# Eight-batch pooled attention and channel mix: longer weight slots, a planner with other rules, and a new order of the first hundred microseconds

## The chip, the cores and the metric

The kernel runs on one core of one Trainium2 chip. The core has a matrix engine (PE, with its weight loads shown as PEld), three engines for elementwise work (DVE, ACT, POOL) and a queue engine (SP) that issues nearly all transfers. The metric is the device time of one execution in microseconds (us); lower is better. The kernel before took 605.85 us, the median of three runs (605.77 to 607.02).

## The reference

```python
# attention, for 8 batches x 8 heads, q/k/v of 576 x 64
k_p = k.reshape(B, H, Sp, pool, D).mean(axis=3)      # 576 keys pooled to 72
v_p = v.reshape(B, H, Sp, pool, D).mean(axis=3)
scores = scale * np.matmul(q, k_p.transpose(0, 1, 3, 2))
attn = softmax(scores)                               # over the 72 pooled keys
x = heads_to_columns(np.matmul(attn, v_p))           # (8, 576, 512)
# channel mix
x_prev = x shifted down by one token, zero at each batch's start
xk = mu_k * x + (1.0 - mu_k) * x_prev
xr = mu_r * x + (1.0 - mu_r) * x_prev
k = np.maximum(xk @ w_k, 0.0)                        # 512 -> 1024
v = k * k @ w_v                                      # 1024 -> 512
r = 1.0 / (1.0 + np.exp(-(xr @ w_r)))                # 512 -> 512
return r * v
```

The three weights arrive as 64-bit floats.

## The kernel before

The 4608 tokens are cut into 12 chunks of 384, and each chunk into 3 tiles of 128 tokens. A tile goes through `softmax` (scores by `products`, maximum, exponential, sum, normalization) and is transposed on PE (`transposed`, `transposed_rest`) for chunks 0 and 1, or through a transfer to DRAM and back for later chunks. A chunk then goes through `attended` (the product with the pooled values), `shifted` (the two mixes, xk and xr), `hidden` (8 column blocks of w_k, relu, square), `gate` (w_r, sigmoid) and `mixed` (w_v, times the gate).

Chunk 0 multiplies with 32-bit weights in PE's plain fp32 form (the tile names begin with got_). Chunks 1 to 11 split weights and operands into a high and a low part and do three faster products in their place (names w_k, w_r, w_v; xkh and xkl). So each of the 20 weight pieces (wk0 to wk7, wr0 to wr3, wv0 to wv7) is first loaded as 64-bit words, then made a 32-bit one by `convert` (a cast on the engine that TOP_BY names, then a DVE operation, line 631), and later split by `split` (HIGH_BY and LOW_BY name the engines).

Keys and values are summed over groups of 8 by `sums`, on PE with the identity (line 672), on DVE or on POOL (SUM_BY). `warm` and `fill` run matmuls whose results nobody reads. BY_HEAD names the tiles whose exponentials are 8 instructions on ACT, each with its own sum (line 817); the others take one DVE subtraction (825), one ACT exponential (830) and one DVE sum (832).

The order of all instructions is made when the kernel is built, by the class `Order`. Every piece of work is a thread with a due time (DUE, by name); a cost model keeps a clock for each engine, estimates when loads land (`fetched`) and how fast PE's clock runs (`stretch`), and always issues, among those that could start about first, the thread that is due first. Nothing of the model is left at run time: each engine executes its list in order and waits on semaphores. Loads leave on SP in the order of LOADS, with eight in flight. A weight piece lies in one of 21 slots: `sb.tile([P, 2 * WP + 1], I32)`, 4100 bytes a partition.

Of the kernel before, what the change touches and what calls it, by code (L numbers as in the profile page):

```python
# [10 lines left out]
I32 = mybir.dt.int32  # L11
# [8 lines left out]
P = 128  # L20
# [11 lines left out]
WP = 512  # L32
# [9 lines left out]
    "k0 k1 q0 q1 wk0 wk1 q2 r0 v0 q4 wr2 v1 v2 q5 wr3 c0 wk7 k2 wk3 wv4 wv6 q3 k3 wk5 wv2 wk2 "  # L42
    "wv7 wv1 v3 wr1 wr0 r1 wv5 wv0 wk4 wv3 wk6 "
)

SUM_BY = {"k0": "t", "k1": "v", "v0": "t", "v1": "t", "r0": "v", "k2": "t", "k3": "t", "v2": "t", "v3": "g", "r1": "g", "k5": "v", "k4": "v", "v5": "v", "r2": "v", "v4": "g"}

NORM_BY = {0: "g", 1: "g", 2: "g", 3: "v", 7: "v", 5: "v", 4: "g", 8: "g", 6: "v"}
# [3 lines left out]
TOP_BY = {"k": "aaaaaaaa", "r": "vvvv", "v": "aaagaaga"}  # L52
HIGH_BY = {"k": "aaaaaagg", "r": "aaga", "v": "gaaaaaga"}
LOW_BY = {"k": "vvgvgggv", "r": "vgvg", "v": "gvvgvvvv"}
BY_HEAD = (0, 1, 5, 7, 8)

SQUARED_ON_ACT = 4
# [27 lines left out]
    "warm": 490.04, "constants": 16.13, "complements": 481.25, "values 2 1": 205.94, "values 2 0": 224.51,  # L85
# [123 lines left out]
class Order:  # L209
# [75 lines left out]
    def stretch(self, at, length):  # L285
# [7 lines left out]
        elif busy > 0.93:  # L293
            self.slow = False
# [1052 lines left out]
```

## Time and profile before

| | |
|---|---|
| median of three runs | 605.85 us |
| the profiled execution | 607.92 us, of which 606.1 us is the span from the first to the last instruction |
| PE busy | 594.3 us, 98% of the span |
| DVE, ACT, POOL busy | 60%, 53%, 34% |
| granted PE clock, mean | 0.994 |
| chain of waits that ended last | PE 86%, DVE 3%, ACT 3%, POOL 2% |

The busy digits of the page stand for 40 equal slices of about 15 us. The granted clock is a share of 2.4 GHz: 1.00 is that level and 0.50 is 1.2 GHz. An idle engine matters only where somebody waits for it. In the first 10 us the clock row prints 0.9 and more whatever PE does; how fast it runs there has to be read from the durations.

### The profile page before, as it was taken

The numbers are of one execution on the slowest core, as the hardware profiler recorded it, in microseconds if no ns is written. First come the engines' busy times: TensorE is split into PE (matmuls) and PEld (weight loads), VectorE is DVE, ScalarE is ACT, GpSimd is POOL, SyncE is SP. The second block draws the span as 40 slices with busy tenths as digits, with TensorE's granted clock in tenths as the row PEclk, the third lists the DMA queues.
The fourth block names the chain that finished last, engine by engine and source line by source line (L and its number), as shares of the span: only waits on it lengthen the run. The fifth ranks groups of instructions, "written<-read, shape, count | busy, mean of one in ns | idle before, by whom it ended". The sixth has DMA issues, their size and how long they took to land.

```text
span 606.1 us, 10539 instructions
## 1 busy us (share of the span) xinstructions
PE 594.3 (98%) x4026; PEld 494.1 (82%) x4026; DVE 362.1 (60%) x738; ACT 318.7 (53%) x670; POOL 207.7 (34%) x295
## 2 busy tenths in 40 slices
PE   7799999999999999999999999999999999999997
PEld 7655545978987988978988988987987988978985
DVE  4688877986985836667936736664864324423411
ACT  4668775575457455565556446365566336344420
POOL 0234338347036228147206208217425006005000
PEclk9979999999999999999999999999999999999999
DMA  9995044358464206416324106424014000000001
GB/s 304 382 379 182 31 158 111 115 151 238 131 160 115 75 32 167 165 72 171 129 79 111 58 21 147 155 92 114 19 41 113 18 1 35 18 0 37 18 1 52
DMA packets 43011, 66.62 MB, mean 110 GB/s; under 512 B 7504, under 2 KB 23120, under 8 KB 42960
## 3 DMA queue, kind: packets, MB, share of 16 engines
q1 hardware_dynamic: 42816, 65.82, 34.6%
q8 instruction: 31, 0.51, 0.4%
q14 instruction: 20, 0.16, 0.1%
q10 hardware_dynamic: 144, 0.13, 0.1%
HBM read 47.65 MB, written 18.28 MB: 109 GB/s over the span
## 4 chain that ended last, share of the span: by engine, by line
PE 86%; DVE 3%; ACT 3%; POOL 2%; issue 1%; DVEq 0%; POOLq 0%; ACTq 0%
PE mm L1126 32%; PE mm L1212 31%; PE mm L1179 15%; PE pair L1038 3%; PE pair L739 2%; PE pair L1019 2%; ACT e L817 1%; POOL xkl L1098 1%; POOL xrl L1098 1%; PE mm L672 1%; ACT turned L622 1%; DVE ptr L974 0%; POOL w_r L657 0%; DVE w_k L657 0%; ACT sh L1139 0%
## 5 line engine op out<-in xcount | busy, mean ns | idle before, releaser
L1126 PE MATMUL mm<-xkh,w_k 128*128 128x384 f32 x704 | 181.7, 339 | 0.0
L1212 PE MATMUL mm<-w_v,sh 128*128 128x512 f32 x528 | 170.5, 397 | 0.0
L1126 PEld LDWEIGHTS mm<-xkh,w_k 128*128 128x128 f32 x704 | 127.5, 188 | 2.3 <-issue 1.0
L1212 PEld LDWEIGHTS mm<-w_v,sh 128*128 128x128 f32 x528 | 99.1, 188 | 27.8 <-issue 5.0
L1126 PE MATMUL mm<-xkl,w_k 128*128 128x384 f32 x352 | 118.7, 337 | 0.3 <-POOL xkl L1098 0.3
L1212 PE MATMUL mm<-w_v,sl 128*128 128x512 f32 x264 | 104.1, 394 | 0.0
L1080 DVE SCALAR_TENSOR_TENSOR xm<-pair,mu_sb,t 128x384 f32<-128x384 f32 x88 | 51.8, 613 | 83.7 <-POOL t L1071 47.3
L1179 PE MATMUL mm<-w_r,xrh 128*128 128x512 f32 x264 | 84.3, 394 | 0.0
L844 POOL TENSOR_TENSOR e<-e,sm 128x576 f32<-128x576 f32 x28 | 33.5, 1206 | 143.9 <-DVE sm L839 99.3
L1139 ACT ACTIVATE rk<-mm 128x384 f32<-128x384 f32 x88 | 43.1, 491 | 70.4 <-PE mm L1126 65.3
L1147 DVE SCALAR_TENSOR_TENSOR rk<-mm,rk 128x384 f32<-128x384 f32 x88 | 48.1, 553 | 35.3 <-ACT rk L1139 35.1
L1126 PEld LDWEIGHTS mm<-xkl,w_k 128*128 128x128 f32 x352 | 66.1, 188 | 0.6 <-POOL xkl L1098 0.6
L1154 ACT CAST sh<-rk 128x384 fp32r<-128x384 f32 x88 | 44.7, 512 | 36.5 <-DVE rk L1147 36.2
L1098 POOL TENSOR_TENSOR xkl<-xm,xkh 128x384 fp32r<-128x384 f32 x44 | 47.7, 1086 | 46.7 <-ACT xkh L1096 46.6
L1060 ACT ACTIVATE t<-pair,om_sb 128x384 f32<-128x384 f32 x96 | 49.3, 580 | 27.4 <-PE pair L1038 26.6
L657 DVE TENSOR_TENSOR sl<-rk,sh 128x384 fp32r<-128x384 f32 x88 | 50.0, 573 | 16.6 <-ACT sh L1154 15.7
L1212 PEld LDWEIGHTS mm<-w_v,sl 128*128 128x128 f32 x264 | 49.5, 188 | 11.3
L1179 PEld LDWEIGHTS mm<-w_r,xrh 128*128 128x128 f32 x264 | 49.6, 188 | 11.1
L1225 DVE TENSOR_TENSOR rs<-mm,rs 128x512 f32<-128x512 f32 (+1 forms) x37 | 24.8, 673 | 56.1 <-PE mm L1212 55.7
L1179 PE MATMUL mm<-w_r,xrl 128*128 128x512 f32 x132 | 52.1, 395 | 0.0
L1098 POOL TENSOR_TENSOR xrl<-xm,xrh 128x384 fp32r<-128x384 f32 x44 | 47.7, 1089 | 5.1 <-ACT xrh L1096 4.8
L657 POOL TENSOR_TENSOR stage<-stage 128x512 f32<-128x512 f32 (+5 forms) x54 | 47.0, 873 | 3.8 <-ACT rs L1185 1.9
(106 smaller groups left out, 710.2 us busy)
## 6 DMA issues: line engine op xcount, KB each, us to landing
qs<-in_qT SPq DMA_DIRECT2D x36, 256.0 KB, 4.5
out<-rs SPq DMA_DIRECT2D x35, 256.0 KB, 2.0
passing<-pm SPq DMA_DIRECT2D x30, 288.0 KB, 2.1
stage<-in_kT SPq DMA_DIRECT2D x14, 576.0 KB, 4.0
turned<-passing SPq DMA_DIRECT2D x40, 192.0 KB, 3.8
stage<-in_vm SPq DMA_DIRECT2D x13, 512.0 KB, 4.1
got_wk<-in_w_k SPq DMA_DIRECT2D x8, 512.0 KB, 8.7
got_wv<-in_w_v SPq DMA_DIRECT2D x8, 512.0 KB, 10.5
```

The source lines that it names most:

```text
L657: (nc.vector if on_vector else nc.gpsimd).tensor_tensor(out=out, in0=a, in1=b, op=op)
L844: eng.tensor_tensor(out=e, in0=e, in1=sm.broadcast_to([P, 2, 4, KEYS]), op=ALU.mult)
L1060: nc.scalar.activation(out=t[:, m, 1:n + 1], in_=xp, func=AF.Copy, scale=om_sb[:, m, g:g + 1])
L1080: nc.vector.scalar_tensor_tensor(out=xm[:, :n], in0=xp, scalar=mu_sb[:, m, g:g + 1], in1=t[:, m, :n], op0=ALU.mult, op1=ALU.add,)
L1098: nc.gpsimd.tensor_tensor(out=lo, in0=xm[:, :n], in1=hi, op=ALU.subtract)
L1126: nc.tensor.matmul(out=hp, lhsT=w[:, o], rhs=x[:, ct, o_t], start=(ct == 0 and k == 0), stop=(ct == NCT - 1 and k == len(terms) - 1),)
L1139: nc.scalar.activation(out=rk[:, :n], in_=hp, func=AF.Relu)
L1147: nc.vector.scalar_tensor_tensor(out=rk[:, :n], in0=hp, scalar=0.0, in1=rk[:, :n], op0=ALU.max, op1=ALU.mult)
L1154: nc.scalar.copy(out=sh, in_=rk[:, :n])
L1179: nc.tensor.matmul(out=bank, lhsT=x[:, ct, o], rhs=w, start=(ct == 0 and k == 0), stop=(ct == NCT - 1 and k == len(terms) - 1),)
L1212: nc.tensor.matmul(out=bank, lhsT=s[:, o], rhs=w, start=(jt == 0 and k == 0), stop=(jt == NJT - 1 and k == len(terms) - 1),)
L1225: nc.vector.tensor_tensor(out=rs[:, o], in0=bank[:, o], in1=rs[:, o], op=ALU.mult)
```

## The change

The slot of a weight piece becomes 2 * WP + 32 words, 4224 bytes. The model in `Order` is changed: loads are limited to eight in flight with another latency, rate and a lag; PE's clock is judged by fixed slices of time, with 64-row matmuls counted as a quarter; clears and the casts of `convert` have other prices. LOADS, the tables that give work to engines, and 171 of 481 due times (those of the first three or four chunks) are replaced, and four due times are new. The other 310 are the same numbers.

```diff
 LOADS = (
-    "k0 k1 q0 q1 wk0 wk1 q2 r0 v0 q4 wr2 v1 v2 q5 wr3 c0 wk7 k2 wk3 wv4 wv6 q3 k3 wk5 wv2 wk2 "
-    "wv7 wv1 v3 wr1 wr0 r1 wv5 wv0 wk4 wv3 wk6 "
+    "k0 k1 q1 wk1 q0 wk0 r0 q5 v0 q2 v1 wr2 v2 wr3 wk7 k2 q4 wv4 c0 wv6 q3 k3 wk3 wv1 wv2 wk5 wk2 wv7 wv3 "
+    "v3 wr1 wr0 wk4 wv5 r1 wv0 wk6 "
 )
-NORM_BY = {0: "g", 1: "g", 2: "g", 3: "v", 7: "v", 5: "v", 4: "g", 8: "g", 6: "v"}
+NORM_BY = {0: "v", 1: "v", 2: "g", 3: "g", 7: "v", 5: "v", 4: "v", 8: "v", 6: "v", 10: "g", 11: "g", 9: "g"}
-TOP_BY = {"k": "aaaaaaaa", "r": "vvvv", "v": "aaagaaga"}
-HIGH_BY = {"k": "aaaaaagg", "r": "aaga", "v": "gaaaaaga"}
-LOW_BY = {"k": "vvgvgggv", "r": "vgvg", "v": "gvvgvvvv"}
-BY_HEAD = (0, 1, 5, 7, 8)
-SQUARED_ON_ACT = 4
+TOP_BY = {"k": "ggagaaaa", "r": "avvv", "v": "vaagaagv"}
+HIGH_BY = {"k": "gaaaaaga", "r": "agaa", "v": "gaaaagaa"}
+LOW_BY = {"k": "vvggvgvg", "r": "vggg", "v": "vvvggvvv"}
+BY_HEAD = (0, 7, 12, 14)
+SQUARED_ON_ACT = 8
 DUE = {
-    "keys 0 0": 144.96, "values 0 0": 154.97, "keys 0 1": 673.65, "values 0 1": 197.76,
+    "keys 0 0": -36.14, "values 0 0": 113.89, "keys 0 1": 721.88, "values 0 1": 519.26, "last_values 0": 287.88,
...
-    WINDOW = 3.4
+    WINDOW = 3.413
+    PHASE = 1.0
+    LAG = 1.7
...
-        self.landed = max(self.now - 0.6 + 2.5, self.landed) + kb / 380.0
-        self.make(what, self.landed)
+        at = self.now
+        if len(self.landings) >= 8:
+            at = max(at, self.landings[-8])
+        self.landed = max(at - 0.6 + 2.25, self.landed) + kb / 400.0
+        self.landings.append(self.landed + (self.LAG if 13 < self.landed < 50 else 0.0))
+        self.make(what, self.landings[-1])
...
-            got = sb.tile([P, 2 * WP + 1], I32, name=f"got_{kind}{i}", tag=f"w{slot}")
+            got = sb.tile([P, 2 * WP + 32], I32, name=f"got_{kind}{i}", tag=f"w{slot}")
```

The first place is PE between the sums of batch 0's values and the first `attended` (L1019 before, L1018 now; every line of the changed file from there on stands one lower). `early_sl`, `early_xrl` and `turned_99` hold raw values and keys, `pm` and `px` are normalized tiles, `pair` holds scores or the attended product. Before:

```order
L672 MATMUL mm_116<-early_sl,ident 128x128 x8
L672 MATMUL mm_114<-early_sl,ident 128x128 x8
L963 MATMUL mm_116<-ident,px_90 64x128
L672 MATMUL mm_115<-early_xrl,ident 128x128 x4
L963 MATMUL mm_114<-ident,px_90 64x128
L672 MATMUL mm_115<-early_xrl,ident 128x128 x4
L926 MATMUL mm_115<-ident,pm_88 128x128 x4
L672 MATMUL mm_117<-turned_99,ident 128x144 x4
L926 MATMUL mm_115<-ident,pm_87 128x128 x4
L672 MATMUL mm_117<-turned_99,ident 128x144 x4
L963 MATMUL mm_115<-ident,px_91 64x128
L926 MATMUL mm_117<-ident,pm_88 128x128 x4
```

and now, the same stretch with the row of scores and the first row of the attended product behind it:

```order
L671 MATMUL mm_116<-early_sl,ident 128x128 x8
L671 MATMUL mm_114<-early_sl,ident 128x128 x8
L671 MATMUL mm_115<-early_xrl,ident 128x128 x8
L962 MATMUL mm_114<-ident,px_90 64x128
L962 MATMUL mm_117<-ident,px_89 64x128
L925 MATMUL mm_115<-ident,pm_88 128x128 x4
L962 MATMUL mm_115<-ident,px_91 64x128
L925 MATMUL mm_114<-ident,pm_88 128x128 x4
L925 MATMUL mm_117<-ident,pm_87 128x128 x4
L671 MATMUL mm_114<-turned_99,ident 128x144 x4
L738 MATMUL pair_113<-ks_69,qs_105 64x72 x16
L1018 MATMUL pair_112<-ptr_316,vbd_r_73 128x384 x2
```

Four of the eight key sums that stood between the transposes have moved behind the first attended product, and the transposes of all three tiles stand together after the value sums.

The second place is ACT from its first weight cast to the copies of the same transposes (L622 and L621 are the cast of `convert`, L817 and L816 the exponentials by head, L971 and L970 copies of the transposed rest, L933 and L932 of the transposed tile). Before:

```order
L622 CAST turned_98<-got_wk_132 128x512
L622 CAST turned_98<-got_wk_135 128x512
L817 ACTIVATE e_85,sm_95<-pair_112,mx_93 128x72 x8
L817 ACTIVATE e_86,sm_96<-pair_113,mx_94 128x72 x8
L703 COPY vs_71<-mm_116 128x128
L830 ACTIVATE e_85<-e_85 128x576
L703 COPY vs_71<-mm_114 128x128
L971 CAST ptr_302<-mm_116 32x128 x2
L971 CAST ptr_302<-mm_114 32x128 x2
L703 COPY vs_72<-mm_115 128x128
L622 CAST turned_98<-got_wk_240 128x512
L980 CAST ptr_302<-mm_114 32x128
```

and now:

```order
L816 ACTIVATE e_85,sm_95<-pair_112,mx_93 128x72 x8
L829 ACTIVATE e_86<-e_86 128x576
L702 COPY vs_71<-mm_116 128x128
L829 ACTIVATE e_85<-e_85 128x576
L702 COPY vs_71<-mm_114 128x128
L621 CAST turned_98<-got_wk_222 128x512
L702 COPY vs_72<-mm_115 128x128
L970 CAST ptr_316<-mm_114 32x128
L970 CAST ptr_316<-mm_117 32x128
L970 CAST ptr_316<-mm_114 32x128
L970 CAST ptr_316<-mm_117 32x128
L932 COPY pt_338<-mm_115 128x4x128
```

The casts of wk0 and wk1 and eight of the sixteen exponentials have left ACT, and the cast of wk7 (got_wk_222, a load) now stands ahead of the last value copy and of all the transposes' copies.

## Rows read from the trace of the kernel before

**Rows 1.** The page: busy time of each engine, and PE's granted clock.
```profile
PE 594.3 (98%) x4026; PEld 494.1 (82%) x4026; DVE 362.1 (60%) x738; ACT 318.7 (53%) x670; POOL 207.7 (34%) x295
...
PEclk9979999999999999999999999999999999999999
```
**Rows 2.** Busy time by stretch: stretch, its length, engines, granted clock, DMA share, GB/s.
```profile
22.50:26.20 3.70, 2.28 (x17) 1.74 (x15) 3.59 (x11) 2.11 (x7) 0.00 (x0) 1.00 1.02 408
26.20:29.60 3.40, 2.30 (x18) 1.92 (x17) 3.32 (x8) 2.91 (x7) 1.79 (x2) 1.00 1.03 400
29.60:33.05 3.45, 1.96 (x44) 1.11 (x42) 2.70 (x6) 2.03 (x8) 0.00 (x0) 1.00 1.04 413
33.05:39.87 6.82, 6.82 (x29) 3.91 (x22) 5.72 (x13) 5.83 (x10) 0.71 (x7) 0.50 1.03 383
39.87:60.00 20.13, 19.88 (x128) 11.97 (x127) 16.75 (x29) 14.33 (x43) 11.01 (x14) 1.00 0.65 232
60.00:150.00 90.00, 89.55 (x651) 62.01 (x650) 72.63 (x145) 58.62 (x141) 46.45 (x59) 1.00 0.45 133
150.00:600.00 450.00, 450.00 (x2939) 392.09 (x2938) 246.86 (x509) 222.63 (x415) 144.43 (x204) 1.00 0.27 79
```
**Rows 3.** PE in order of time to 62 us: start, length, instruction, idle before.
```profile
3.08 2.08 PE L524 MATMUL mm<-turned 128*128 128x256 f32 x4 [3.08 <-DVE turned L520]
4.94 4.05 PE L672 MATMUL mm<-stage,ident 128*128 128x144 f32 x16
...
9.93 1.23 PE L739 MATMUL pair<-ks,qs 64*64 64x72 f32 x64
11.09 4.73 PE L540 MATMUL mm<-ident 128*128 128x128 f32 x40
15.75 0.73 PE L739 MATMUL pair<-ks,qs 64*64 64x72 f32 x32
...
18.93 2.05 PE L672 MATMUL mm<-early_sl,ident 128*128 128x128 f32 x16 [0.47 <-DMA early_sl<-in_vm]
...
27.53 1.15 PE L672 MATMUL mm<-turned,ident 128*128 128x144 f32 x8
...
31.98 0.62 PE L1019 MATMUL pair<-ptr,vbd_r 96*128 96x384 f32 x2 [0.86 <-ACT ptr L980]
...
38.08 2.42 PE L1126 MATMUL mm<-xkh,got_wk 128*128 128x384 f32 x4
...
56.78 5.43 PE L1126 MATMUL mm<-xkh,got_wk 128*128 128x384 f32 x16 [0.25 <-DVE sh L1147]
```
**Rows 4.** ACT in order of time to 64 us, same columns.
```profile
12.32 0.32 ACT L817 ACTIVATE e<-pair,mx 128x72 f32<-128x72 f32 x1 [0.70 <-DVE mx L813]
...
16.78 0.41 ACT L817 ACTIVATE e<-pair,mx 128x72 f32<-128x72 f32 x1
...
23.59 0.77 ACT L622 CAST turned<-got_wk 128x512 f16<-128x512 bf16 x1 [0.30 <-DMA got_wk<-in_w_k]
...
25.81 0.26 ACT L980 CAST ptr<-mm 32x128 fp32r<-32x128 f32 x1
...
26.40 0.59 ACT L933 COPY pt<-mm 128x512 f32<-128x512 f32 x1
```
**Rows 5.** DVE in order of time to 64 us, same columns.
```profile
2.54 0.48 DVE L520 MEMSET turned<- 128x512 f32 x1
...
27.20 1.60 DVE L722 TENSOR_TENSOR vbd_r<-vq,mask_sb 96x256 fp32r<-96x256 f32 x2
```
**Rows 6.** PE in order of time from 60 to 160 us, same columns.
```profile
84.02 0.69 PE L1019 MATMUL pair<-ptr,vbd_r 96*128 96x192 f32 x4 [0.19 <-ACT e L817]
...
104.92 0.44 PE L1126 MATMUL mm<-xkl,w_k 128*128 128x384 f32 x1 [0.26 <-POOL xkl L1098]
```
**Rows 7.** ACT in order of time from 64 to 92 us, same columns.
```profile
71.26 1.28 ACT L1185 ACT_TABLE_LOAD   x1
72.55 0.60 ACT L1185 ACTIVATE rs<-mm 128x512 f32<-128x512 f32 x1
```

More of the change, by code (lines that the diff above doesn't have):

```diff
@@ L41 @@
 LOADS = (
-    "k0 k1 q0 q1 wk0 wk1 q2 r0 v0 q4 wr2 v1 v2 q5 wr3 c0 wk7 k2 wk3 wv4 wv6 q3 k3 wk5 wv2 wk2 "
-    "wv7 wv1 v3 wr1 wr0 r1 wv5 wv0 wk4 wv3 wk6 "
-)
-SUM_BY = {"k0": "t", "k1": "v", "v0": "t", "v1": "t", "r0": "v", "k2": "t", "k3": "t", "v2": "t", "v3": "g", "r1": "g", "k5": "v", "k4": "v", "v5": "v", "r2": "v", "v4": "g"}
-NORM_BY = {0: "g", 1: "g", 2: "g", 3: "v", 7: "v", 5: "v", 4: "g", 8: "g", 6: "v"}
+    "k0 k1 q1 wk1 q0 wk0 r0 q5 v0 q2 v1 wr2 v2 wr3 wk7 k2 q4 wv4 c0 wv6 q3 k3 wk3 wv1 wv2 wk5 wk2 wv7 wv3 "
+    "v3 wr1 wr0 wk4 wv5 r1 wv0 wk6 "
+)
+SUM_BY = {"k0": "t", "k1": "v", "v0": "t", "v1": "t", "r0": "v", "k2": "t", "k3": "t", "v2": "t", "v3": "v", "r1": "g", "k5": "v", "k4": "v", "v5": "v", "r2": "v", "v4": "g"}
+NORM_BY = {0: "v", 1: "v", 2: "g", 3: "g", 7: "v", 5: "v", 4: "v", 8: "v", 6: "v", 10: "g", 11: "g", 9: "g"}
 WARMING = 4
 FILLS = ((("scored", 1), 20),)
-TOP_BY = {"k": "aaaaaaaa", "r": "vvvv", "v": "aaagaaga"}
-HIGH_BY = {"k": "aaaaaagg", "r": "aaga", "v": "gaaaaaga"}
-LOW_BY = {"k": "vvgvgggv", "r": "vgvg", "v": "gvvgvvvv"}
-BY_HEAD = (0, 1, 5, 7, 8)
-SQUARED_ON_ACT = 4
+TOP_BY = {"k": "ggagaaaa", "r": "avvv", "v": "vaagaagv"}
[3 more added lines that the diff above has]
+SQUARED_ON_ACT = 8
 REST_BY = (1, 1, 3)
@@ L62 @@
 DUE = {
[22 rows of a table removed]
-    "warm": 490.04, "constants": 16.13, "complements": 481.25, "values 2 1": 205.94, "values 2 0": 224.51,
[17 rows of a table removed]
[22 rows of a table added]
+    "warm": 525.34, "constants": -181.8, "complements": 1678.53, "values 2 1": -741.97, "values 2 0": 598.55,
[15 rows of a table added]
     "x_parts 3 2 1 0": 735.71, "x_parts 3 3 0 0": -119.85, "x_parts 3 3 1 0": -10.57, "hidden 3 0 0": 6.06,
@@ L105 @@
     "split_turned 6": 410.72, "split_turned 7": 501.45, "split_turned 8": 495.95, "split_turned 9": 313.38,
-    "free_turned": 478.83, "fetch_turned 2": 92.93, "split_turned 10": 300.71, "split_turned 11": 198.56,
[14 rows of a table removed]
+    "free_turned": 478.83, "fetch_turned 2": -381.2, "split_turned 10": 300.71, "split_turned 11": 198.56,
[12 rows of a table added]
     "softmax 27": -756.46, "scores 9": 168.64, "softmax 28": 531.98, "softmax 29": 732.89,
@@ L218, in __init__ @@
         self.landed = 0.0
+        self.landings = []
         self.now = 0.0
@@ L224, in __init__ @@
         self.mode = "whole"
-        self.slow, self.bursts = True, []
+        self.busy = {}
         self.counts = {}
@@ L283, in advance, with stretch @@
                 return
-    def stretch(self, at, length):
+    def stretch(self, at, length, mode):
         if at > 60:
             return length
-        self.bursts = [b for b in self.bursts if b[1] > at - self.WINDOW]
-        busy = sum(b[1] - max(b[0], at - self.WINDOW) for b in self.bursts) / self.WINDOW
-        if busy < 0.39:
-            self.slow = True
-        elif busy > 0.93:
-            self.slow = False
-        length *= 1 + self.slow
-        self.bursts.append((at, at + length))
+        k = int((at + self.PHASE) / self.WINDOW)
+        if self.busy.get(k - 1, 0.0) < 0.6:
+            length *= 2
+        weight = 0.25 if mode == "quarters" else 1.0
+        end = at + length
+        while at < end:
+            until = min(end, (k + 1) * self.WINDOW - self.PHASE)
+            self.busy[k] = self.busy.get(k, 0.0) + weight * (until - at) / self.WINDOW
+            at, k = until, k + 1
         return length
@@ L332, in run @@
                     length, self.mode = length + self.CHANGE[mode], mode
-                length = self.stretch(at, length)
+                length = self.stretch(at, length, mode)
             elif func and func[0] and func[0] != self.table:
@@ L518, in warm @@
         zeros = yield take("tmp")
-        yield "dve", 0.6, False
+        yield "dve", 0.5, False
         nc.vector.memset(zeros, 0.0)
@@ L528, in cleared @@
     def cleared(i):
-        yield "dve", 0.6, False
+        yield "dve", 0.5, False
         nc.vector.memset(tops[i], 0.0)
@@ L614, in convert @@
         got = held.pop(("got", kind, i))
-        words = got[:, 1:].rearrange("p (n two) -> p n two", two=2)[:, :, 0]
-        first = got.bitcast(BF16)[:, 2:].rearrange("p (n four) -> p n four", four=4)[:, :, 2]
+        words = got[:, 1:2 * WP + 1].rearrange("p (n two) -> p n two", two=2)[:, :, 0]
+        first = got.bitcast(BF16)[:, 2:4 * WP + 2].rearrange("p (n four) -> p n four", four=4)[:, :, 2]
         top = yield take("tmp")
@@ L620, in convert @@
         if by == "a":
-            yield act(WP)
+            yield "act", 0.62, False
             nc.scalar.copy(out=upper, in_=first)
         elif by == "g":
-            yield pool(WP)
+            yield "pool", 0.91, True
             nc.gpsimd.tensor_copy(out=upper, in_=first)
         else:
-            yield dve(WP)
+            yield "dve", 0.42, True
             nc.vector.tensor_copy(out=upper, in_=first)
```

223 rows, old and new, of the table DUE are left out of this document.

## The prediction

> **What bounds the kernel now.** I read the page first, then the busy time by stretch, then PE in order of time with its waits, and last the engines that PE waits for. The page shows PE busy for 594.3 of 606.1 us [rows 1], so all that can be won without less work on PE is the 11.8 us in which it is idle and the time that a low clock adds to its work. The stretches say where these lie: from 150 to 600 us PE is busy to the last hundredth, from 60 to 150 us it misses 0.45 us, from 39.87 to 60 us 0.25 us. From 22.5 to 33.05 us it misses 1.42, 1.10 and 1.49 us, and from 33.05 to 39.87 us it never rests but is granted half the clock [rows 2]. At 2.4 GHz that work would have taken 3.41 us less. With the 3.08 us before PE's first matmul [rows 3], the first 40 us hold nearly everything. The transfers move 400 to 413 GB/s up to 33 us [rows 2]: what comes off the memory late there can't come sooner, only in another order.
>
> The clock has a second place. Before 9 us, 8 sums of 144 columns take 4.05 us, 0.51 each, and later 4 take 1.15, 0.29 each [rows 3]. PE thus also starts at the lower level, whatever the clock row prints there.
>
> **The change part by part.** The longer slot adds and removes no instruction, and the planner's new rules act only through the order. I cost both at 0. The casts and DVE operations on a slot might change with its address; bounds for that are 0 and the loads' conversions up to 40 us getting a tenth faster or slower, 0.08 us in each 0.77 us cast [rows 4], which ACT's waits hide. PE's work is the same set of matmuls in both. The sum is therefore one of waits and clock, and I follow PE through the new list, with the durations of before.
>
> *Start.* The clear that PE waits for is third of four now; each takes 0.48 to 0.53 us (the fourth begins at 2.54 [rows 5]). PE begins at 2.55 instead of 3.08 us. But three warming matmuls, not two, stand before the key sums, at some 0.9 us each, so the sums begin at 5.25 instead of 4.94. One, not two, follows them: the first scores come at 9.7 instead of 9.93 us. Gain 0.2.
>
> *Scores of the third tile.* They need the first pair of banks, which ACT frees when its exponentials by head are done: 16 of them start every 0.30 us from 12.32 to 16.78 [rows 4]. The change leaves 8. The bank is free at 14.6 us; 16 of the 20 fill matmuls, 0.23 us each, end then too; the scores come at 14.7 instead of 15.75 [rows 3]. The other 4 fills (0.93) follow. v1 is now loaded ahead of wr2, 0.52 MB or some 1.3 us earlier, so the 0.47 us wait for it [rows 3] goes. The 24 sums of values end at 22.3 us; before they end, two short transposes included, at 23.0. Gain 0.7.
>
> *The transposes, from 22.3 us to the first attended product.* This is where the new list is most exposed, because ACT works in order and the cast of wk7 now stands before the last value copy. Before, that cast began at 23.59, ended by its load [rows 4]. The order of loads puts one q tile (0.26 MB) less ahead of it, 0.65 us at 408 GB/s [rows 2], so it begins at 22.9. The chain: cast to 23.55 (starts of such casts lie 0.65 apart), value copy 23.8, so PE waits 1.35 for the bank; first transposes to 24.35; four copies of 0.26 and the tile copy of 0.59 [rows 4] to 25.4, PE waits 1.0; DVE's subtractions and ACT's third copies free the next bank at 26.15, PE waits 0.55; two tiles to 27.15; two copies, the cast of wv4 and the tile copy to 28.1, PE waits 0.9; four key sums (1.0) and scores (0.7) to 29.8; the pair of vbd_r products, 0.8 each [rows 5], whose first is ready at 30.05, wait 0.25. Together 4.05 us of waiting, against 4.0 before; but the attended product begins at 30.05 instead of 31.98 [rows 3], since four key sums went behind it and the sums ended 0.7 earlier.
>
> *From there to the hidden layer.* Two attended products (0.55 + 0.8 each at the full level) with 12 key sums between and after (0.245 each): first hidden matmul at 35.6 instead of 38.08 [rows 3], with all 16 key sums done instead of 12. Lead: 2.5 + 1.0 = 3.5. Before then loses 0.9 more, half of 38.08 to 39.87 at half clock, and 0.25 at 56.78 [rows 3]. The new list gives back about 0.6, because wk2 is wanted after four matmuls (2.5 us) and its bank waits for ACT's key copy at 38.7. Lead without any fall of the clock: 3.5 + 0.9 + 0.25 - 0.6, about **4.0 us**.
>
> *Does the clock fall?* Before, the fall at 33.05 follows 3.45 us in which PE was idle 1.49 and for the rest partly on 64-row matmuls, while 1.42 idle of 3.70 and 1.10 of 3.40 were still borne [rows 2]. In my chain PE is idle 2.9 us between 22.3 and 26.15. I expect a fall near 26. It may cost little: half the matmuls under it run where PE would wait anyway (0.5 us), or, when it lasts into the attended products, as much as before, 3.4. I take half of that, 1.7.
>
> The Trainium skill, page "TensorE: Matmul & The Clock Gate", section "What's actually happening", says the chip's check of activity runs freely and isn't started by the kernel. That speaks against the new planner rule, which fixes the check's phase to the program's start; the one profiled execution can't show it. By the rule the fall would lie elsewhere in other executions, and the sum would scatter between the two ends above rather than be 2.3.
>
> *Later.* Squares of chunk 0 move to ACT entirely (8 instead of 4), four more normalizations to DVE. PE's next narrow place is the second attended product at 84.02, which waited 0.19 for ACT's exponentials, and the first low parts of xk, which POOL gave 0.26 late at 104.92 [rows 6]. In the new list the whole of the first group of four xkl is wanted right after the mixed products, but POOL's list up to the fourth is some 13 us of work where 18 us passed before, and PE needs it some 19 us after the attended product. I cost it at 0, bounds -0.5 and +4 (the slower rival).
>
> **Sum:** -4.0 + 1.7 = -2.3 us on the span. The profiled execution took 607.92 us, span 606.1 and 1.8 around it; the change acts in the span, so I take it off the median of the runs, 605.85, which is 2.07 below the profiled one: **603.5 us**.
>
> **Rivals.**
> *The clock holds.* Then -4.0, and 0.9 more if it also rises before the key sums end, which PE's start half a microsecond earlier favours: 601.8 down to 601.0. For it: the new order puts 128-row sums between the 64-row products, where before the clock was low. Against it: the idle 2.9 us above.
> *The same time.* The fall costs all of its 3.4 us again, or a wait of mine is a microsecond longer in two places: -0.6, 605.2, with ends at 604.6 and 607. For it: all of the stretch's waits stand behind in-order casts that wait for loads, and I took each load's latency from a single one of before.
> *Slower: ACT reaches the second attended product late.* Before, its exponentials there ended with the wait of 0.19. The new list puts another table load (1.28) and sigmoid (0.6) [rows 7], two casts, copies of the sixth tile (0.26 + 0.59) and of keys (0.3) between these exponentials and that product: 4 us in all. I count 1.1 us of slack, if ACT has nothing left over when the first gate bank is done. If it comes 4 us or more late there, PE loses at least 2.9, and the time is 606.5 and beyond, about 607.5 with a fallen clock. It decides from 3.4 us of lateness on.
> *Nothing arrives.* If the last weights, the same bytes in total, set the end of chunk 0, no lead survives. Against it: before, PE's only wait after 40 us was 0.25 us, for a bank and not for a load [rows 3].
>
> **How the numbers follow.** Forecast, 602.0 to 604.6: 0.50. Clock holds, below 602.0: 0.14. Same, with the case of the last weights, within 0.2% or 1.2 us of 605.85 (about what a measurement of this kernel can tell from no change): 0.22. Slower: 0.14. So faster 0.64, same 0.22, slower 0.14. The range from 601.2 to 606.8 leaves out about 0.08 below and 0.12 above.
>
> **What would show it.** In the new profile: PE's first matmul near 2.55, third scores near 14.7, value sums ended near 22.3, first attended product near 30, first hidden matmul between 35.6 and 37.3; one stretch of clock 0.50 beginning near 26 rather than at 33; ACT waiting for the load of wk7; no new wait over 1 us from 40 to 150 us. The prediction is wrong if the attended product doesn't start before 31.5, if clock 0.50 lasts as long as before, or if PE waits for ACT or POOL at the second attended product or at the first xkl.

## The result, and the profile after

The changed kernel took 599.99 us, the median of four runs (599.77 to 601.05), against 606.43 us for the kernel before in the runs beside it (605.77 to 607.12): a ratio of 0.990 (0.988 to 0.992), or 6.4 us faster. The forecast was 603.5 us with a range from 601.2 to 606.8: the sign was right, the size less than half of what came. The profiled execution took 599.92 us, of which 598.1 us is the span. One execution of the kernel before, of 654.95 us at a mean granted clock of 0.849, stands in none of the figures.

PE in order of time (start, length, instruction, idle before), the rows that answer to [rows 3] and [rows 6]; line numbers are one lower than before:

```profile
2.53 2.93 PE L523 MATMUL mm<-turned 128*128 128x256 f32 x6 [2.53 <-DVE turned L519]
5.25 2.92 PE L671 MATMUL mm<-stage,ident 128*128 128x144 f32 x16
...
8.95 1.23 PE L738 MATMUL pair<-ks,qs 64*64 64x72 f32 x64 [0.35 <-DMA qs<-in_qT]
...
14.92 0.73 PE L738 MATMUL pair<-ks,qs 64*64 64x72 f32 x32 [0.97 <-DMA qs<-in_qT]
...
20.15 1.95 PE L671 MATMUL mm<-early_xrl,ident 128*128 128x128 f32 x16
...
23.89 0.27 PE L962 MATMUL mm<-ident,px 128*64 128x128 f32 x1 [0.78 <-ACT pt L932]
24.69 1.06 PE L925 MATMUL mm<-ident,pm 128*128 128x128 f32 x8 [0.52 <-ACT ptr L979]
26.59 1.25 PE L671 MATMUL mm<-turned,ident 128*128 128x144 f32 x8 [0.84 <-ACT pt L932]
...
28.43 0.62 PE L1018 MATMUL pair<-ptr,vbd_r 96*128 96x384 f32 x2
...
34.30 6.79 PE L1125 MATMUL mm<-xkh,got_wk 128*128 128x384 f32 x20
...
60.68 3.70 PE L1178 MATMUL mm<-got_wr,xrh 128*128 128x512 f32 x8 [0.55 <-ACT sh L1138]
```

The first attended product (L1018) starts at 28.43 instead of 31.98 us, the first hidden matmul (L1125) at 34.30 instead of 38.08 [rows 3]. Between 22 and 30 us PE waits 0.78 + 0.52 + 0.84 = 2.14 us. Busy time by stretch (columns as in [rows 2]) shows the clock at its full level where it was at half before, and after 60 us one wait of 0.55 us:

```profile
22.50:26.20 3.70, 1.95 (x13) 1.34 (x13) 2.98 (x9) 3.52 (x13) 1.04 (x1) 1.00 1.04 401
26.20:29.60 3.40, 3.01 (x50) 2.12 (x50) 3.13 (x9) 2.02 (x6) 0.04 (x1) 1.00 1.03 406
29.60:33.05 3.45, 3.45 (x30) 2.47 (x26) 2.51 (x5) 2.73 (x6) 0.94 (x3) 1.00 1.03 410
33.05:39.87 6.82, 6.82 (x29) 4.29 (x26) 6.28 (x13) 3.57 (x9) 2.77 (x8) 1.00 1.02 405
...
60.00:150.00 90.00, 89.45 (x577) 64.82 (x576) 70.91 (x145) 63.19 (x155) 47.09 (x59) 1.00 0.44 137
```

All of that lies ahead of the second chunk. But the lead still grows where both kernels keep PE busy without a gap. The first matmul of the gate in chunk 1 and in the last chunk, in the profile before and after:

```profile
119.96 0.39 PE L1179 MATMUL mm<-w_r,xrh 128*128 128x512 f32 x1
...
577.33 0.39 PE L1179 MATMUL mm<-w_r,xrh 128*128 128x512 f32 x1
```
```profile
113.30 0.40 PE L1178 MATMUL mm<-w_r,xrh 128*128 128x512 f32 x1
...
569.46 0.40 PE L1178 MATMUL mm<-w_r,xrh 128*128 128x512 f32 x1
```

The lead is 119.96 - 113.30 = 6.66 us at the first and 577.33 - 569.46 = 7.87 us at the second: 1.21 us come over 457 us in which PE waits for nothing in either kernel, so no order matters any more. Nothing in the forecast could make that. The second thing to see: the two profiled spans differ by 8.0 us, the medians by 6.4. The profile before was of an execution 2 us slower than the median, and the forecast read its durations from it.

### The profile page after: what moved, and what is told of

Same layout as the page of the kernel before. It is cut to its first block, busy times and chain, and to the rows that moved or that the text cites. A ratio compares the mean times of both kernels' runs of the same rounds, so it can differ in the third digit from the quotient of the medians.

```text
span 598.1 us, 10517 instructions
## 1 busy us (share of the span) xinstructions
PE 587.9 (98%) x4026; PEld 491.4 (82%) x4026; DVE 360.6 (60%) x743; ACT 319.5 (53%) x657; POOL 206.0 (34%) x291
## 4 chain that ended last, share of the span: by engine, by line
PE 94%; DMA 3%; ACT 1%; DVE 1%; SPq 1%; issue 0%; DVEq 0%; ACTq 0%
PE mm L1211 34%; PE mm L1125 33%; PE mm L1178 17%; PE pair L738 3%; PE pair L1037 3%; PE pair L1018 2%; DMA got_wk<-in_w_k 2%; DMA qs<-in_qT 1%; PE mm L671 1%; SPq L603 0%; SPq L589 0%; DVE stage L656 0%; ACT turned L621 0%; ACT ptr L970 0%; DVE ptr L973 0%
## 5 line engine op out<-in xcount | busy, mean ns | idle before, releaser
L1125 PE MATMUL mm<-xkh,w_k 128*128 128x384 f32 x704 | 180.7, 338 | 0.0
L1125 PEld LDWEIGHTS mm<-xkh,w_k 128*128 128x128 f32 x704 | 127.4, 188 | 1.8 <-issue 0.5
L1125 PE MATMUL mm<-xkl,w_k 128*128 128x384 f32 x352 | 118.4, 336 | 0.0
L1125 PEld LDWEIGHTS mm<-xkl,w_k 128*128 128x128 f32 x352 | 66.1, 188 | 0.0
L656 POOL TENSOR_TENSOR stage<-stage 128x512 f32<-128x512 f32 (+5 forms) x51 | 44.6, 876 | 5.8 <-DMA stage<-in_vr 4.1
```

The lines of the kernel that those rows point to most:

```text
L656: (nc.vector if on_vector else nc.gpsimd).tensor_tensor(out=out, in0=a, in1=b, op=op)
L1125: nc.tensor.matmul(out=hp, lhsT=w[:, o], rhs=x[:, ct, o_t], start=(ct == 0 and k == 0), stop=(ct == NCT - 1 and k == len(terms) - 1),)
```

## The experiments

Kernels measured together ran on one chip with runs of the kernel before among them; the ratio is to those, with its 95% interval. The kernel before took 606.03 us beside e1 and 607.01 beside e9 to e12, so versions that did not run together are best compared by their ratios. In e1 and e3 to e12 every engine's list is that of the changed kernel except for what the edit names.

**e1. The changed kernel again.** 

> The changed kernel once more, as the measure for the runs beside it. If its lead is the plan's own (the order of loads and instructions), it is again about 1.0% faster than the kernel before, 599.8 to 600.2 us with an occasional execution a microsecond longer, PE's first matmul at 2.53, the cast of wk7 near 21.4 and no stretch at half clock between 10 and 597 us. If the first profile of it was a lucky execution (transfers that ran undisturbed, a clock that happened to hold), the times scatter by 1 to 3 us and the trace shows a stretch at 0.50 or a cast of wk7 well after 21.4.

599.88 us (599.70 to 600.72), ratio 0.990 (0.989 to 0.991). The plan's own lead, then. But the profiled execution was the longest of the four (600.72 us), and its trace has the fall of the clock that the first had not; the stretch:

```profile
26.53:29.94 3.41, 3.41 (x41) 2.99 (x41) 1.71 (x5) 1.60 (x5) 0.37 (x1) 0.50 1.03 406
```

The same list, the same waits (one of 0.18 us came on top), half the clock for 3.41 us, 0.8 us lost (600.72 - 599.92).

Executions without a trace tell it by their mean granted clock, which is on record for each. In the profiles 0.999 and 1.000 go with no stretch at 0.50 before the last 10 us, 0.997 with one of 3.41 us, 0.993 and 0.994 with 6.83 us. Taking 0.997 and less for a fall, two of the changed kernel's eight executions had a fall, 601.05 and 600.72 us, both at 0.997; the six others took 599.70 to 600.06. Of the 47 executions of the kernel before that ran beside the experiments, 35 had one.

**e2. The longer slot alone, in the kernel before.** 

> The kernel before with the weight slots 128 bytes longer and nothing else. Theory: the slot's length is worth nothing, ratio 1.000 within 0.1%, and the casts stay at 0.77 us. Rival: part of the 6 us comes from the slot's place in memory; then this alone is 0.2% or more faster, and casts, or the transfers between 13.5 and 17 us (219 and 176 GB/s for 1 us each in the profile before), are quicker. Its trace also tells whether those slow transfers belong to the old order of loads (they come back, and the cast of wk7 starts near 23.6 again) or to that one execution (the cast starts about 1.1 us earlier, near 22.5, and half of my error on the loads was a reading from a disturbed trace).

```diff
-            got = sb.tile([P, 2 * WP + 1], I32, name=f"got_{kind}{i}", tag=f"w{slot}")
+            got = sb.tile([P, 2 * WP + 32], I32, name=f"got_{kind}{i}", tag=f"w{slot}")
```

604.16 us (603.42 to 604.55), ratio 0.9967 (0.9955 to 0.998): 2.0 us faster. The rival holds, but not by its reasons. The cast of wk7 takes what it took, 0.77 us. What is quicker is PE, in the stretch in which it never waits:

```profile
117.74 0.40 PE L1179 MATMUL mm<-w_r,xrh 128*128 128x512 f32 x1
...
573.48 0.39 PE L1179 MATMUL mm<-w_r,xrh 128*128 128x512 f32 x1
```

455.74 us from one to the other, where the kernel before takes 577.33 - 119.96 = 457.37: 1.63 us less for the same list. This trace also shows what in the profile before belonged to that one execution. The transfers from 13.5 to 17 us, issued in the same order, run at 363 GB/s here and not at 251. The slots don't explain it by themselves: e5 has the short ones too and moves 407 GB/s there. The stretch in the profile before, in this one and in the changed kernel's, and ACT in this one:

```profile
13.50:17.00 3.50, 3.50 (x58) 3.30 (x58) 0.60 (x3) 3.50 (x26) 1.30 (x2) 1.00 0.99 251
```
```profile
13.50:17.00 3.50, 3.50 (x58) 3.30 (x57) 1.26 (x3) 3.50 (x25) 1.29 (x2) 1.00 1.02 363
```
```profile
13.50:17.00 3.50, 2.53 (x49) 2.29 (x48) 2.88 (x9) 1.09 (x5) 0.00 (x0) 1.00 0.99 396
```
```profile
22.76 0.77 ACT L622 CAST turned<-got_wk 128x512 f16<-128x512 bf16 x1
```

The cast starts at 22.76, with no wait for its load, against 23.59 [rows 4]. And there is no stretch at half clock before 600 us in this execution (by the mean clock four of the six have one): that, too, comes and goes with the same list.

**e3 and e4. The load of wk7 later in the changed kernel**, behind k2, and behind k2, q4 and wv4. Only SP's list changes.

```diff
+HELD, BEHIND = ("wk7",), "k2"      # e4: "wv4"
...
+    def start_load(what, out, in_):
+        if what in HELD:
+            postponed.append((out, in_))
+            return
+        nc.sync.dma_start(out=out, in_=in_)
+        if what == BEHIND:
+            for o, i in postponed:
+                nc.sync.dma_start(out=o, in_=i)
...
-            nc.sync.dma_start(out=qs, in_=qT[i])
+            start_load(f"q{i}", qs, qT[i])
...
```

> The changed kernel, every engine's list as it is, but the load of wk7 issued behind the load of k2 (0.59 MB, 1.45 us at 405 GB/s). The cast of wk7 then starts near 22.85 us, which is what the prediction had assumed. Theory (the prediction's chain is right and only its arrival times were wrong): PE's waits between 22 and 30 us grow from 2.1 to about 3.6 to 4 us, the first attended product starts at 29.9 to 30.1, and the time is 1.4 to 1.7 us above the changed kernel without a fall of the clock, about 3 above it with one. Rival (ACT's list has slack there, PE is held by something else): the attended product starts before 29 and the time is less than 0.5 us above.

> As the run before, but the load of wk7 issued behind k2, q4 and wv4 (1.37 MB, 3.4 us). The cast of wk7 then starts near 24.8. Theory that idleness of PE makes the clock fall: PE stands idle for over 4 of the 8 us from 21.9 to 30, more than the kernel before had, a stretch at 0.50 follows within a few microseconds in every profile, and the time is 5 us or more above the changed kernel (3.4 of waiting, 1.7 to 3.4 of clock). Rival that the clock falls by chance or by something else than the idle time: no stretch at 0.50, and the time is about 3.4 above.

e3: 602.09 us (600.38 to 603.41), ratio 0.993 (0.991 to 0.995); e4: 604.67 us (603.01 to 606.60), 0.9976 (0.9963 to 0.9989). PE waits for the value copy that stands behind the cast in ACT's list, in e3 and then in e4 (lines stand twelve lower there: L937 is L925, L1030 is L1018):

```profile
23.89 0.65 PE L937 MATMUL mm<-ident,pm 128*128 128x128 f32 x4 [1.33 <-ACT vs L714]
...
31.35 0.62 PE L1030 MATMUL pair<-ptr,vbd_r 96*128 96x384 f32 x2
```
```profile
25.56 0.66 PE L937 MATMUL mm<-ident,pm 128*128 128x128 f32 x4 [3.32 <-ACT vs L714]
```

In e3 the attended product starts at 31.35 where e1, with a fall at nearly the same place, has 29.84: 1.5 us for a cast 1.56 us later (22.95 against 21.39). So the chain of the forecast (load, cast, value copy, bank) is the one that binds there, and only its starting time was wrong. The whole time follows less closely: e3's two executions without a fall took 600.38 and 600.43 us, some 0.5 above the changed kernel's and not the 1.4 to 1.7 expected; they have no trace, so how late wk7 came in them isn't known. In e4 the median is 4.8 us above e1's, near the 5 expected with a fall of the clock. Its profile, the fastest of twelve executions, has 3.41 us at 0.50 (mean clock 0.997); the eleven others have 0.994 or 0.992, so longer or repeated falls. No execution of e4 was without one.

**e5, e6, e11, e12. The slot's place.** The built kernel gives the addresses: with the short slot, 4128 bytes after rounding, starts cycle through 0, 32, 64 and 96 bytes past a 128-byte line; with the long one all stand 64 past it. e5 takes the changed kernel back to the short slot, e6 to one 64 bytes longer (0 and 64 in turn), e11 and e12 keep the length and shift nearly all slots by 32 and 64 bytes (all but one at 96, all but one at 0). The operands that these weights are multiplied with start 64 bytes past a 128-byte line in all of them.

```diff
-            got = sb.tile([P, 2 * WP + 32], I32, ...)
+            got = sb.tile([P, 2 * WP + 1], I32, ...)     # e5; e6: 2 * WP + 16
+    sb.tile([P, 8], F32, name="ahead")                   # e11; e12: 16 words
...
+            if (kind, i) == ("wk", 6):
+                held["behind"] = sb.tile([P, 24], F32, name="behind")    # e12: 16 words
```

> The changed kernel with the weight slots 4 bytes longer again instead of 128, every engine's list the same. Theory (PE reads weights a little slower from slots that start 32 bytes off a 64-byte line, as eleven did before; shown by a lead of the slot-only kernel that grows evenly from 2.22 us at 120 us to 3.86 at 580): 1.5 to 1.8 us above the changed kernel, 601.4 to 601.7, the lead over it lost evenly over 120 to 580 us, and the mean of the matmuls on w_k, w_r and w_v 1 to 2 ns higher. Rival (the slot helped the old order only, by the transfers or casts before 40 us): equal to the changed kernel within 0.3 us.

> The changed kernel with the weight slots 64 instead of 128 bytes longer: every slot starts on a 64-byte line, every second one now on a 128-byte line. Theory that only the 32-byte offset costs: equal to the changed kernel within 0.2 us. Rival that it is the 128-byte line that counts, or that all slots have one and the same offset: 0.8 us or more to either side.

> The changed kernel, slots of the same length, all twenty but one moved by 32 bytes so that each starts 96 bytes past a 128-byte line; the operands of the channel mix stay where they were. Theory (an offset of 32 from a 64-byte line costs PE some 1 to 3 ns in each matmul on such a slot): about twice what the short slot lost, where half of them had it: 2 to 5 us above the changed kernel, lost evenly from 120 to 590 us. Rival (what costs is that slots have different offsets): within 0.3 us of the changed kernel over that stretch.

> The same with the slots moved by 64 bytes: all but one start on a 128-byte line instead of 64 past one. Theory (the offset from a 64-byte line is what counts, and equal offsets are equal): within 0.3 us of the changed kernel over 120 to 590 us. Rival (a start on the 128-byte line costs, as half the slots of the 64-byte version had it and lost 0.85 us): 1 to 2 us above, lost evenly.

The time from the first gate matmul of chunk 1 to that of the last chunk, read as above:

| slots start past a 128-byte line by | kernel | from, to (us) | length | PE's waits in it | against 64 everywhere, without the waits | ratio of the run |
|---|---|---|---|---|---|---|
| 64 | changed | 113.30, 569.46 | 456.16 | 0 | 0 | 0.990 |
| 0 and 64 | e6 | 113.92, 570.89 | 456.97 | 0 | +0.81 | 0.9923 (0.9911 to 0.9936) |
| 0 | e12 | 114.20, 571.27 | 457.07 | 0.38 | +0.53 | 0.991 (0.989 to 0.993) |
| 96 | e11 | 116.37, 574.04 | 457.67 | 0 | +1.51 | 0.9932 (0.9916 to 0.9949) |
| 0, 32, 64, 96 | e5 | 113.45, 571.85 | 458.40 | 0.21 | +2.03 | 0.9941 (0.9926 to 0.9955) |

The same stretch takes 456.04 us in each of the seven other profiles that have this list and all slots at 64 (e1, e3, e4, e7 to e10). So it repeats to 0.12 us, whatever happened before it, and every row of the table stands clear of that.

Rows of e5, the second with its one wait, and the wait of e12:

```profile
113.45 0.40 PE L1178 MATMUL mm<-w_r,xrh 128*128 128x512 f32 x1
...
147.83 0.62 PE L1125 MATMUL mm<-xkh,w_k 128*128 128x384 f32 x2 [0.21 <-DVE rk L1146]
...
571.85 0.40 PE L1178 MATMUL mm<-w_r,xrh 128*128 128x512 f32 x1
```
```profile
148.71 0.62 PE L1129 MATMUL mm<-xkh,w_k 128*128 128x384 f32 x2 [0.38 <-DVE rk L1150]
```

e5 settles the size: 602.62 us (601.79 to 604.16), 0.4% of the ratio or 2.5 us above the changed kernel, 2.24 of it in this stretch, where 2.03 are lost while PE works without a gap. Over the 2,040 matmuls on these slots in the stretch that is 1 ns each. The reason that I gave for it is only half of the truth. Moving all slots 32 bytes off costs less than the mixture, not twice as much, and a start on the 128-byte line costs 0.5 us, which I had expected to cost nothing; two starts mixed (e6) cost more than either alone. In the whole time the 0.5 us can't be seen: e12's two executions without a fall took 599.90 and 599.93 us, as the changed kernel's do. That the place of the slots sets the rate is shown; which rule on the address lies behind it stays open.

**e7. PE half a microsecond later.**

```diff
-        nc.vector.memset(zeros, 0.0)
+        _ = [nc.vector.memset(zeros, 0.0) for _ in range(2)]
```

> The changed kernel with the clear that PE waits for done twice, so that PE's first matmul comes at 3.05 us as before and not at 2.53; nothing else. Theory (the clock at the start rises at an edge that each execution has elsewhere, and the start is hidden behind loads): the key sums end between 8 and 9 us, the first scores wait 0 to 0.2 us less for their q tile, and the time is 0 to 0.5 us above the changed kernel. Rival (the earlier start makes the clock rise some 2 us sooner, which the trace of the changed kernel suggested with sums of 2.92 instead of 4.05 us): 1 us or more above.

601.69 us (599.84 to 602.84), ratio 0.992 (0.9905 to 0.994). The first matmul came at 3.19, and the first scores waited for nothing. The two executions without a fall took 599.84 and 600.46 us, so the later start can be hidden; the four with one took 601.65 to 602.84, and the median is 1.8 us above. The profile is of the slowest. In it the load of wk7 came late (the cast at 22.57 and not at 21.39, with the transfers at 335 GB/s from 13.5 to 17 us), PE waited 1.04 us for the value copy behind that cast, and the clock fell for 6.82 us. ACT, PE and the stretch:

```profile
22.57 0.76 ACT L621 CAST turned<-got_wk 128x512 f16<-128x512 bf16 x1 [1.80 <-DMA got_wk<-in_w_k]
```
```profile
23.51 0.66 PE L925 MATMUL mm<-ident,pm 128*128 128x128 f32 x4 [1.04 <-ACT vs L702]
```
```profile
26.42:33.24 6.82, 6.24 (x54) 4.02 (x52) 4.93 (x12) 2.85 (x7) 0.76 (x1) 0.50 1.02 406
```

On the clock the rival has a point. The record of the granted clock begins at 9.35 us here, and at 9.15 to 9.31 in the three other profiles with PE's start at 3.07 or 3.08 us (before, e2, e13); with the start at 2.53 or 2.54 it begins at 5.71 to 8.08 (twelve profiles). On the time neither theory is out: what the half microsecond costs hangs on the clock and the loads of the execution.

**e8. Two waits away.** A version meant to be faster than the changed kernel: `q5 v0 q2` becomes `q2 v0 q5` in LOADS, and the cast of wk7 is issued on GpSimd.

> A version meant to beat the changed kernel: q2 is loaded ahead of v0 and q5 behind it (third scores waited 0.97 us for q2), and the cast of wk7 goes to GpSimd, which stands idle from 11.4 to 21.5 us, so that ACT's last value copy no longer stands behind it. Theory: the third scores start near 14.0 instead of 14.92, the last value copy near 21.1 to 21.4 instead of 22.14, PE's waits between 22 and 27 us fall from 2.1 to under 1.5 us, and the time is 0.5 to 1.5 us below the changed kernel. Rival (what stands behind, the normalized probabilities of tiles 0 to 2 from DVE and GpSimd, is late as well, or PE is then idle elsewhere before 30 us): within 0.3 us of it.

600.60 us (600.43 to 601.77), ratio 0.991 (0.990 to 0.993): the rival. The third scores now wait for the exponentials by head and not for q2, the last value copy comes at 21.77, and PE still waits 0.78 + 0.96 = 1.74 us at the next two places, against 2.14 at three and the 1.5 hoped for:

```profile
14.55 0.73 PE L738 MATMUL pair<-ks,qs 64*64 64x72 f32 x32 [0.42 <-ACT e L816]
...
23.52 0.27 PE L962 MATMUL mm<-ident,px 128*64 128x128 f32 x1 [0.78 <-ACT pt L932]
24.75 1.86 PE L925 MATMUL mm<-ident,pm 128*128 128x128 f32 x8 [0.96 <-ACT ptr L979]
```

The load of wk7 has not left the path, it has changed engines. GpSimd's cast waits for it, DVE's half of `convert` (L630) for the cast, the subtractions of the transposes (L973) stand behind that in DVE's list, and ACT's last copies (L979) wait for them. GpSimd, DVE and ACT:

```profile
21.53 0.76 POOL L621 CAST turned<-got_wk 128x512 f16<-128x512 bf16 x1 [9.69 <-DMA got_wk<-in_w_k]
```
```profile
22.32 0.74 DVE L630 SCALAR_TENSOR_TENSOR got_wk<-got_wk,turned 128x512 int32<-128x512 int32 x1 [0.72 <-POOL turned L621]
```
```profile
23.89 0.88 ACT L979 CAST ptr<-mm 32x128 fp32r<-32x128 f32 x4 [0.51 <-DVE ptr L973]
```

The 0.3 us won ahead of them was won with a fall of the clock (24.85 to 28.26) in its profile. All five executions had a fall (mean clock 0.994 to 0.997); four took 600.43 to 600.79, where the changed kernel's two with a fall took 600.72 and 601.05.

**e9 and e10. Work in PE's waits.** Fill matmuls ahead of the waits after 23 us, eight in the changed kernel and seven in e8's.

```diff
+    BURN = {("rest", 2): 3, ("main", 2): 2, ("keys", 1, 0): 3}      # e10: 3, 4, 0
+    def burn(*what):
+        for _ in range(BURN.pop(what, 0)):
+            nc.tensor.matmul(out=order.slots["pair"][0][1][:, 0, :P], lhsT=ident, rhs=ident, start=True, stop=True)
...
+        burn("main", i)      # and ("rest", first), ("keys", b, p), each ahead of its matmuls
```

> The changed kernel with eight more fill matmuls (0.23 us each) in PE's list where it waits between 22.9 and 26.6 us: three ahead of the wait of 0.78, two ahead of that of 0.52, three ahead of that of 0.84. They write a bank that nobody reads then. Theory (it is PE's idle time there that lets the clock fall in some executions): no stretch at 0.50 before 590 us, all times within 0.4 us of 599.8, none a microsecond above. Rival (the fall comes from what stands in the lists elsewhere, or by chance): a stretch at 0.50 near 25 to 30 us in the profile or times at 600.5 to 601 in a quarter or more of the executions, as without the fills.

> The version with q2 ahead of v0 and the cast of wk7 on GpSimd, with seven fill matmuls ahead of its two waits (0.78 and 0.96 us). That version measured 600.6 us and had a stretch at 0.50 from 24.85 to 28.26 in its profile. Theory (the two moves do gain some 0.3 us, and a fall of the clock took it back): no stretch at 0.50, 599.3 to 599.7 us, the fastest of all. Rival (nothing was gained ahead of the attended products): 599.8 us or more, with no stretch at 0.50 either.

e9: 601.40 us (600.64 to 602.48), ratio 0.9915 (0.990 to 0.993); e10: 602.27 us (600.52 to 603.36), 0.9925 (0.991 to 0.994). The clock held in both profiles, and by its mean (0.999 or 1.000) in all 11 executions. Of the 31 executions of the changed kernel and of e5, e6, e11 and e12, which have its list without the fills, 13 had a fall. So that half of e9's theory holds. Of e9 (L739 is L738, L1027 is L1018) the filled waits, and the wait that spoils the time:

```profile
15.59 0.73 PE L739 MATMUL pair<-ks,qs 64*64 64x72 f32 x32 [1.45 <-DMA qs<-in_qT]
...
23.61 0.83 PE L921 MATMUL pair<-ident 128*128 128x128 f32 x6
...
27.26 1.25 PE L672 MATMUL mm<-turned,ident 128*128 128x144 f32 x8 [0.18 <-ACT pt L940]
...
29.10 0.61 PE L1027 MATMUL pair<-ptr,vbd_r 96*128 96x384 f32 x2
```

q2 came 0.7 us later than in the changed kernel's profile, with the same loads ahead of it, and that is still there at 29.10. In e10 it is the load of wk7, 1.06 us later than in e8, and the chain shown there carries it to PE. GpSimd, DVE and PE of e10:

```profile
22.59 0.77 POOL L621 CAST turned<-got_wk 128x512 f16<-128x512 bf16 x1 [10.71 <-DMA got_wk<-in_w_k]
```
```profile
23.39 0.75 DVE L630 SCALAR_TENSOR_TENSOR got_wk<-got_wk,turned 128x512 int32<-128x512 int32 x1 [1.00 <-POOL turned L621]
```
```profile
25.82 1.06 PE L933 MATMUL mm<-ident,pm 128*128 128x128 f32 x8 [0.85 <-ACT ptr L988]
```

So the half of the theory on times fails: with the clock steady the times still scatter by 1.8 us (e9) and 2.8 (e10). Part of that lies outside the span, which is 598.9 to 599.7 and 598.7 to 600.7 us: in six of the 11 executions 2.2 to 3.3 us stand around it and not the usual 1.8, and why isn't known. No version here beat the changed kernel.

**e13 and e14. Loads and lists apart.** The kernel before with the longer slots and the new LOADS; the changed kernel with the old LOADS. The planners and tables are their own, so all lists are laid out again.

> The kernel before with the longer slots and the new order of loads; its planner, tables and due times are the old ones, and plan around the new arrivals. Theory (most of the 4 us that the order is worth comes from what the loads bring earlier): 601 to 602.5 us, against 604.2 with the longer slots alone. Rival (the loads' order helps only together with the lists that were laid out for it): 603.5 to 606 us, with new waits of PE before 45 us in the trace.

> The changed kernel with the old order of loads; its planner, tables and due times are the new ones. Theory (loads first): the cast of wk7 starts near 22.8 to 23.6 again and the time is 602 to 604 us. Rival (lists and loads are worth something only together): 604 us or more, at or above the kernel before. If it stays under 601.5 us the lists alone bring the gain, and the loads little.

620.07 us (619.83 to 620.22), ratio 1.0225 (1.021 to 1.024), and 623.28 us (622.39 to 624.17), 1.028 (1.026 to 1.030): 14 and 17 us slower than the kernel before. The rivals hold in that loads and lists help only together, far beyond the size I gave them, and not at the place: e13's was to show ahead of 45 us, where its new waits are 1.20 us at most. PE's longest waits, in order of time, of e13 and of e14:

```profile
100.59 0.69 PE L1019 MATMUL pair<-ptr,vbd_r 96*128 96x192 f32 x4 [3.38 <-DVE e L825]
...
107.08 0.69 PE L1126 MATMUL mm<-xkl,w_k 128*128 128x384 f32 x1 [3.58 <-POOL xkl L1098]
...
117.78 0.44 PE L1126 MATMUL mm<-xkl,w_k 128*128 128x384 f32 x1 [4.13 <-POOL xkl L1098]
```
```profile
154.86 1.72 PE L738 MATMUL pair<-ks,qs 64*64 64x72 f32 x48 [5.13 <-DVE xm L1079]
...
161.67 1.72 PE L738 MATMUL pair<-ks,qs 64*64 64x72 f32 x48 [5.09 <-DVE xm L1079]
```

They lie long after the last weight has arrived, at the second attended product, at the first low parts and in the scores of a later chunk, where the two parents wait 0.3 us at most. The clock falls behind them as well (0.50 from 101.47 to 111.71 us in e13, from 152.48 to 169.55 in e14). The due times are tuned to one order of loads; that with another the planner puts other work ahead of what PE needs fits these waits, but which due time is at fault was not tested. How much of the 4 us belongs to the loads can't be had by swapping them.

## Why the prediction was wrong

The forecast for the execution was -4.0 us for the order, +1.7 for a fall of the clock, and 0 for the slot.

**The step that failed** is the sentence "The longer slot adds and removes no instruction [...] I cost both at 0", with bounds for casts and DVE alone. PE does 2,244 matmuls on the same slots in chunks 1 to 11, and I bounded no change there. It is worth 2.0 us in the old order (e2) and 2.5 in the new (e5). With this term alone the forecast becomes 601.0 to 601.5, at the lower end of the range (601.2); without the 1.7 for the clock as well it is 599.3 to 599.8, and 599.99 came.

**The clock** was the second. "I take half of that, 1.7" charged every execution with a fall. The place was right (26.5 us, where I had said "near 26"), but the fall comes in some executions: of the changed kernel's eight, 599.70 to 600.06 six times without one and 600.72 and 601.05 with one, and the one of these with a trace shows it, at 0.8 us. The median bears none, so the rival that the clock holds, which I had given 0.14, is what came; its 601.0 to 601.8 less the slot's 2.0 to 2.5 is 598.5 to 599.8. Executions without a fall take 599.88 us in the median against 605.64 for the 12 such ones of the kernel before, 5.8 us; the rest of the 6.4, some 0.6, is that falls have become rarer, 2 of 8 (13 of 31 with e5, e6, e11 and e12) after 35 of 47.

Five profiles have the changed kernel's waits of 0.78, 0.52 and 0.84 us to 0.01 us (it, e1, e5, e6, e12). What tells them apart is where the records of the granted clock begin at the start: at 6.87 and 7.88 us (changed kernel, e5) the clock held later, at 6.05 to 6.28 (e1, e6, e12) it fell at 26.5 to 26.8. With more waiting there (2.66 to 4.63 us in e3, e4, e7 and e11) or a longer single wait (0.96 in e8) it fell wherever it had risen, from 6.01 to 9.35; with the waits filled, e10 held it though it had risen at 6.31. So idle PE time and the clock's place in the execution decide together, as far as twelve profiles can show it. The Trainium skill, page "TensorE: Matmul & The Clock Gate", section "What's actually happening", says that the check runs freely and isn't started by the kernel. The rises at 5.71 to 8.08 us, with PE's start at 2.53 or 2.54 in each, agree. That the four profiles with a start at 3.07 to 3.19 all have it at 9.15 to 9.35 would be chance by that rule, and four are too few to say. A plan with a fixed phase can't foresee a rise that moves by 2.4 us; less waiting makes the fall rarer, as the 0 of 11 with the waits filled show.

**The order** came out as sized: -3.6 us (e5 against the kernel before, both with short slots, 602.62 and 606.26) to -4.1 (e1 against e2, 0.990 / 0.9967), where I had -4.0. By its steps:

| step | forecast | measured |
|---|---|---|
| PE's first matmul | 2.55 | 2.53 |
| first scores | 9.7 | 8.95, the key sums at the full level from 6.87 on |
| third scores | 14.7, by the bank | 14.92, by the load of q2 |
| sums of values end | 22.3 | 22.1 |
| cast of wk7 | 22.9 | 21.39 |
| PE's waits up to the attended product | 4.05 | 2.14 |
| first attended product | 30.05 | 28.43 |
| first hidden matmul | 35.6 without a fall | 34.30 |
| wait for wk2's matmuls | about 0.6 given back | none |

PE's waits came out 1.9 us shorter than in my chain, because the cast of wk7 came at 21.39 and not at 22.9; e3, with the cast at 22.95, gives 1.33 us of them back (1.33 + 0.78 + 0.53 + 0.83 = 3.47). The arrivals were read from an execution whose transfers had a hole (251 GB/s where e2 has 363): with the same order of loads e2 has that cast at 22.76, 0.83 us ahead of [rows 4]. My sentence on 400 to 413 GB/s holds from 22.5 us on, where those rows begin. The other 0.7 us isn't accounted for; c0 also went behind wk7 in the new LOADS, which I didn't count. Against this stood two credits that the profile before earned and not every execution does: 0.9 for its half clock after 38 us, and its late start of the hidden layer, which e2 shows to cost less (36.81 us without a fall, after a wait of 2.05 for xkh, against 38.08). So -4.0 was right partly by offsetting errors.

Of the rivals, ACT late at the second attended product (slower) didn't come: PE waits for nothing there, and its only wait after 40 us is the 0.55 at 60.68. Nor did the last weights bind.

## What to carry to other kernels

When a change moves a buffer, ask for every reader of it and not only for who fills it, above all for the engine that never rests: 1 ns in each of 2,244 matmuls was a third of this change's gain (2.0 to 2.5 of 6.4 us). Before durations are taken from a profile, hold its time against the median; 2 us more is a sign that some of its waits are that execution's own. A tuned plan is one piece: its loads without its due times, or the reverse, cost 14 to 17 us.

## What the runs showed of the hardware that was not expected

PE's rate depends on where its weights start in memory. With all slots 64 bytes past a 128-byte line the same matmuls take 456.04 to 456.16 us (eight profiles); without PE's waits they take 456.69 us with all slots on the line, 457.67 with all 96 past it and 458.19 with the four starts mixed.

With PE starting at 2.53 or 2.54 us each time, the clock's rise at the start moves between 5.71 and 8.08 us from execution to execution; in five profiles with the same waits the stretch at half clock at 26.5 us came with the rises at 6.05 to 6.28 and not with those at 6.87 and 7.88. Matmuls that nobody reads, put into PE's waits, kept the clock up in 11 of 11 executions, where it fell in 13 of 31 without them.

Transfers issued in the same order ran at 251 GB/s in one execution and at 363 in another from 13.5 to 17 us (the slots differed, but with the short ones e5 moved 407 there), and a q tile came 0.7 us later in e9 than in the changed kernel's profile, in both cases early enough in the kernel for PE to wait for it or for what hangs on it.
